# One core, attention plus product-key experts: when weight halves are split and slots are worked off

## The chip, the cores and the metric

The kernel runs on one core of one Trainium2 chip. The metric is the time of one execution on the device in microseconds. Engines are named as in the profile: PE is TensorE (PEld its weight loads), DVE is VectorE, ACT is ScalarE, POOL is GpSimd, SP is SyncE, which here only issues DMAs.

## What is computed

With `xn = layernorm(x)` for x of 2,048 tokens by 512, the output is `x + A(xn) + B(xn)`. A is attention with 32 query heads of 16 and one shared key and value head, and an output projection. B is a product-key mixture of experts:

```
q1, q2 = split(xn @ w_q)                      # 32 heads, 128 + 128
s1, s2 = q1 @ k1.T, q2 @ k2.T                 # 64 scores each
t1, i1 = top 2 of s1;  t2, i2 = top 2 of s2
cand, eidx = t1[a] + t2[b], i1[a]*64 + i2[b]  # 4 candidates
top_s, top_e = top 2 of cand
g = softmax(top_s)
act = gelu(xn . u[top_e])                     # u, v: 4096 x 512
B = sum over heads and k of g * act * v[top_e]
```

Each token uses 64 of the 4,096 experts.

## The kernel before

**Tokens and stages.** Tokens lie in 16 tiles of 128, four tiles to a group. For groups 0 and 1 the experts' rows are gathered; for groups 2 and 3 all experts are computed densely and weighted by gates that are zero where a token does not use an expert. Products run in float16 as a high and a low half; `TERMS` (L208) lists the three products kept: high by high, high by low, low by high.

**The outer loop.** After a start stage, attention runs in 256 steps (loop at L1582, `att_steps` at L1382). A step does four score products with their exponentials on ACT (L448, L455), 16 recorded matmuls of probabilities by values (L465), and around them the work of the other threads. In a step `mid()` comes first (what was put off to ACT and DVE: `ON_ACT`, `LATER`, `LAST`, `BEHIND`, then dots, sums and gathers of slots), then the second pair of scores, then `fill()`, which runs the score thread until a cost planned for this step is used up. `STORES` are run at the head of the next step, so that what is stored inside a store comes two steps later. Every engine works its instructions off in the order in which this loop writes them; nothing reorders them.

**The score thread** (`score_thread`, L1296) goes through the chunks of `SEQ` (L676): a phase (token group) and one of eight chunks of four heads. In phase 0 the folded weights of a chunk (`w_q` times keys) are made first by `wp_make` (L630): transposes into a PSUM tile of `xtile` (tag x, three buffers in all), the high half by ACT (L659), the low half by DVE (L660). Later phases read them back from DRAM a chunk ahead. `item` (L681) does one tile of tokens for one chunk: 12 matmuls (L699) into an `xtile`, then MAX8 and FIND_INDEX8 on DVE (L712, L714). After four items `batch` (L731) turns the two best into gates and expert numbers: sums and the comparison on DVE (L739 to L745), the exponential on ACT one step later, then the gates on DVE (`gates`, L808 to L817 for the dense phases); the expert numbers on POOL, through `G_` (L757). For the dense phases (`ph >= NSP`) this index chain is 15 instructions (L758, L796 to L799 twice, L801 to L806), and its results `df1` and `df2` are transposed on PE by `spread` (L937).

**The dense part** (`dense`, L824) follows the last chunk of phases 2 and 3. It transposes the expert numbers and gates (`spread(0)`, `spread(1)`, then, when the gates have been written, `spread(2)`; L949 to L954). Then 32 groups of 16 token columns (`q`, NQ = 32) form the dense gates: DVE builds one-hot matrices (`onehot`, L969 to L976), PE multiplies them (L1012), ACT and DVE copy out in turn. `dense_on` is 2 in this stage. Then come 32 blocks of 128 experts: 12 matmuls with a block's u half (`activations`, L911), gelu and gate on ACT and DVE (L1107 to L1132), and every four blocks the sums with the v halves (`sums`, L1047; matmuls L1058). Between blocks 2 and 4 up to three output blocks of attention (`block_out`, L559) are put in. `dense_on` is 3 from near the end of the one-hot stage, 1 from block 4 on.

**Splitting.** In phase 2 a block's rows of u and v come by `fetch` (L829; tile `rw`, two buffers) on SP, and are split by `half_split` (L867): a high half on ACT (L874), a low half on DVE (L877), and a store for phase 3, which reads the halves back (L870) instead. `half(b)` puts off the u half of block b to the next `mid()`, `later_split(b)` what is left of it; the latter also queues the rows of block b + 2 two stores later. `SPLITS` (L980) says at which group q which of these is called; later blocks are split from the block loop. A block whose halves are not there makes the score thread stop for the step (L1077). The gates' rows are read back by `first_gates` and `fetch_gates` on SP (L859, L861).

**Slots.** A slot is one gathered pair of u and v rows for a tile of 128 tokens: a gather by POOL (L1180), a dot on DVE (L1192), four small DVE instructions and one tanh for each four slots, and a sum into the tile's accumulator on DVE (L1227). There are 512. How many are due by a step is `pos`, which grows each step by a rate that depends on `dense_on` (L1587 to L1590):

```
if dense_on[0] == 1:
    pos += 2.5 if d < half * 3 // 4 else max(0.0, NSL - pos) / max(half - 3 - d, 1)
else:
    pos += (2.5 if len(IDX) < NC * TPH else 2.3 if 0 <= d - since < 32 else 1.75, 0, 0.5, 1.5, 0.5)[dense_on[0]]
```

`d` is the step, `half` is 256, and `since` is the last step with a dense part. So the rate is 2.5 in phase 0 and in the blocks, 1.75 in scoring, 2.3 in the 32 steps of scoring after a dense part, 0.5 in the one-hot stage; from step 192 on what is left is spread over the steps that are left.

Of the kernel before, what the change touches and what calls it, by code (L numbers as in the profile page):

```python
# [23 lines left out]
P = 128  # L24
# [9 lines left out]
NC = 8  # L34
TPH = GT
NPH = NGRP
NSP = 2
# [23 lines left out]
def tile_kernel(ctx, tc, x, wq, wkv, wo, wqT, kT, uv, ub, vb, out):  # L61
    nc = tc.nc
# [72 lines left out]
    XT, XS, XK, XN, ACC, XP = [], {}, {}, {}, {}, [None]  # L135
# [70 lines left out]
                BULK.append(lambda k=k, xt=xt: nc.sync.dma_start(d_xt[g - 1][k], raw(xt[:])))  # L206

    TERMS = ((0, 0), (0, 1), (1, 0))  # L208

    FIRST = ((0, 0), (1, 0), (0, 1))  # L210
    cols = const.tile([P, 40], F32, name="cols")
# [383 lines left out]
    WC = {}  # L595
# [85 lines left out]
    def item(n_, ti, make=()):  # L681
        ph, c = SEQ[n_]
        nph, nc_ = SEQ[n_ + 1] if n_ + 1 < len(SEQ) else (None, None)
        t = TPH * ph + ti
        g, j = divmod(t, GT)
        b, jb = divmod(ti, BT)
        if jb == 0:
            m8 = small.tile([P, BT, 8, 8], F32, name="m8", bufs=1)
            i8 = small.tile([P, BT, 8, 8], U32, name="i8", bufs=1)
            M8[ph, c, b], I8[ph, c, b] = m8, i8  # L690
        m8, i8 = M8[ph, c, b], I8[ph, c, b]
        p = xtile("psc")

        more = nc_ is not None and not (ph >= NSP and c == NC - 1)
        read = more and n_ + 1 >= NC
        n = 0
        for k in range(KC):
            for a, bb in TERMS:
                nc.tensor.matmul(p, XT[k][:, a, j * P:(j + 1) * P], WC[n_][k][:, bb, :],  # L699
                                 start=n == 0, stop=n == 11)  # L700
# [12 lines left out]
        for s in range(8):  # L713
            nc.vector.max_index(i8[:, jb, s, :], m8[:, jb, s, :], p[:, s * E:(s + 1) * E])  # L714
        if jb == BT - 1:
            batch(ph, c, b)
        yield 3 * UNIT
# [13 lines left out]
    def batch(ph, c, b):  # L731
# [22 lines left out]
            LATER.append(go)  # L754

        fi = T("fi", F32, [P, BT, 8, 2])
        G_ = nc.gpsimd  # L757
# [66 lines left out]
    def dense(DG, after):  # L824
# [144 lines left out]
        def onehot(q):  # L969
            if q < NQ:  # L970
# [9 lines left out]
        SPLITS = {NQ - 18: lambda: later_split(0), NQ - 15: lambda: later_split(1),  # L980
                  NQ - 12: lambda: half(2), NQ - 10: lambda: later_split(2),
                  NQ - 8: lambda: half(3), NQ - 6: lambda: later_split(3),
                  NQ - 4: lambda: half(4), NQ - 2: lambda: later_split(4)}

        def first_gates():

# [87 lines left out]
        for b in range(NB):  # L1074
            wd = []
            if b > 1:
# [6 lines left out]
                for k in activations(b, splits[b][0], p):  # L1083
                    if k == 0:
                        store(lambda b=b: (fetch_gates(b + 1), fetch_gates(b + 2)))
                        if b % 2 == 0 and b > 2:
# [64 lines left out]
            if b % 2 and b > 1:  # L1151
# [423 lines left out]
    with tc.manual_schedule(engines=ENGINES):  # L1575
# [6 lines left out]
        for d in range(half + 24):  # L1582
# [2 lines left out]
            if dense_on[0] != 0:  # L1585
                since = d
            if dense_on[0] == 1:  # L1587
                pos += 2.5 if d < half * 3 // 4 else max(0.0, NSL - pos) / max(half - 3 - d, 1)
            else:
                pos += (2.5 if len(IDX) < NC * TPH else 2.3 if 0 <= d - since < 32 else 1.75, 0, 0.5, 1.5, 0.5)[dense_on[0]]  # L1590

            todo = max(min(int(pos + 0.001), g_next[0]) - d_next[0], 0) if d else 0

# [109 lines left out]
```

## Time and profile before

| what | value |
|---|---|
| three runs | 1809.59, 1810.92, 1815.26 us (median 1810.92) |
| profiled execution | 1814.29 us |
| its span, first to last instruction | 1812.6 us |
| mean granted TensorE clock | 0.985 |
| HBM read, written | 407.36 MB, 56.39 MB |

In time, by the trace: the first attention step's values start at 123 us, the first one-hot stage runs from about 571 to 663, its blocks to about 1025, scoring to about 1345, the second one-hot stage from 1361 to 1445, its blocks to about 1784.

How to read the rows: a row of busy times by stage gives the stretch in us and its length, then for each engine the busy time and the number of instructions in parentheses, the granted clock of TensorE, the busy share of the DMA engines and the GB/s. A row of waits gives the engine and its instruction, what it waited for, the sum of us, how often, and the longest. A row of the timeline gives start, length, engine, line, operation, written and read tiles, and how many instructions were merged; in brackets the idle time before it and what ended it. A row of groups gives a line's instructions with their count, the busy time and mean ns of one, and the idle time ahead of them.

### The profile page before, as it was taken

Reading aid. Unit: us, or ns where it says so; the run is one execution under the profiler, and the core shown is the slowest. Engines: PE = TensorE matmul, PEld = TensorE weight load, DVE = VectorE, ACT = ScalarE, POOL = GpSimd, SP = SyncE. Lnnn points to the kernel's source line nnn. Section 1 sums busy time; section 2 is a strip of 40 time slices with the busy share of each in tenths; the row PEclk is TensorE's granted clock in tenths of the full one; section 3 lists DMA queues with packets and bytes.
Section 4 is the critical chain, followed back from the end, with each engine's and each line's share of the span. In section 5 each row is a group of like instructions: output and inputs, shape, how many; then the busy total and the mean of one; then the engine's idle time right before and its main releaser. Section 6 shows DMA issues by size and latency. Waiting matters only on the chain.

```text
span 1812.6 us, 35046 instructions
## 1 busy us (share of the span) xinstructions
PE 1705.5 (94%) x11070; PEld 601.1 (33%) x11070; DVE 1592.4 (88%) x6337; ACT 1328.8 (73%) x1793; POOL 685.1 (38%) x923
## 2 busy tenths in 40 slices
PE   7989998999998889999999999999998899999998
PEld 3433332333333332333333333332333333333332
DVE  7748898999998976899899899999989868989995
ACT  6467787877767886888888666655667877777774
POOL 1034353445543012344344455445541124544440
PEclk9999999999999999999999999999998999999999
DMA  7378788999764567899999976777443789999893
GB/s 260 125 254 308 264 279 282 316 321 324 270 212 139 169 230 260 284 313 341 302 334 345 330 280 237 237 245 245 149 159 131 224 263 293 324 292 332 290 311 114
DMA packets 257273, 470.98 MB, mean 260 GB/s; under 512 B 107316, under 2 KB 118596, under 8 KB 257084
## 3 DMA queue, kind: packets, MB, share of 16 engines
q0 software_dynamic: 73728, 268.47, 43.2%
q1 hardware_dynamic: 182940, 199.59, 34.4%
q8 instruction: 87, 1.43, 0.3%
q14 instruction: 102, 0.84, 0.1%
q10 hardware_dynamic: 416, 0.66, 0.1%
HBM read 407.36 MB, written 56.39 MB: 256 GB/s over the span
## 4 chain that ended last, share of the span: by engine, by line
PE 58%; DVE 20%; ACT 8%; issue 3%; DMA 3%; POOL 1%; SPq 0%; ACTq 0%; DVEq 0%; another core or an unknown queue 0%; POOLq 0%
PE pv L465 17%; PE sc L448 10%; PE psc L699 10%; PE pout L1058 8%; PE pact L915 7%; ACT pt L455 5%; DVE i L714 4%; DVE xa L1227 3%; DVE m L712 3%; DVE g L1192 3%; PE pwo L565 2%; DVE oh L973 2%; PE pw L644 1%; ACT wk L874 1%; DMA rsb<-dinv 1%
## 5 line engine op out<-in xcount | busy, mean ns | idle before, releaser
L455 ACT ACTIVATE pt<-sc 128x1024 f32<-128x1024 f32 x1024 | 990.1, 1026 | 336.6 <-PE sc L448 299.2
L1180 POOL DMA_INDIRECT g<-in_uv_dram,idx x512 | 544.6, 1064 | 896.7 <-DVE xa L1227 367.8
L465 PE MATMUL pv<-pt,vaug 128*32 128x512 f32 x4096 | 503.6, 610 | 0.0
L1227 DVE SCALAR_TENSOR_TENSOR xa<-g,w,xa 128x512 f32<-128x512 f32 x512 | 372.2, 745 | 0.0
L699 PE MATMUL psc<-wk,xt 128*128 128x512 f16 x1536 | 358.4, 381 | 12.5 <-DVE i L714 7.2
L448 PE MATMUL sc<-qa,kaug 64*128 64x512 f16 x2048 | 325.6, 385 | 40.0 <-ACT pt L455 35.3
L1192 DVE CUSTOM_DVE_ANT_0 g<-g,xa 128x512 f32<-128x512 f32 x512 | 334.3, 682 | 2.6 <-DMA g<-in_uv_dram,idx 2.6
L699 PEld LDWEIGHTS <-xt 128*128 128x128 f16 x1536 | 140.9, 98 | 210.9 <-issue 63.0
L448 PEld LDWEIGHTS <-kaug 64*128 64x128 f16 x2048 | 82.0, 94 | 381.7 <-issue 377.9
L714 DVE FIND_INDEX8 i<-m,psc 128x8 uint32<-128x64 f32 x1024 | 206.4, 222 | 0.0
L465 PEld LDWEIGHTS pv<-pt,vaug 128*32 128x32 f32 x4096 | 108.2, 110 | 259.8 <-issue 259.8
L915 PE MATMUL pact<-xt,wk 128*128 128x512 f16 x768 | 184.3, 385 | 4.2 <-DVE wk L877 3.9
L1058 PE MATMUL pout<-wk,wd 128*128 128x512 f16 x768 | 176.5, 380 | 0.0
L712 DVE MAX8 m<-psc 128x8 f32<-128x64 f32 x1024 | 146.1, 214 | 7.9 <-PE psc L699 7.2
L915 PEld LDWEIGHTS <-wk 128*128 128x128 f16 x768 | 69.6, 99 | 105.3 <-issue 29.3
L1058 PEld LDWEIGHTS <-wd 128*128 128x128 f16 x768 | 73.2, 98 | 93.3 <-issue 9.3
L973 DVE TENSOR_TENSOR oh<-io,tr 128x2048 f16<-128x2048 f16 x64 | 77.9, 1218 | 10.0 <-PE pg L1012 4.7
L714 DVE MATCH_VALUE_LOAD i<-m,psc 128x8 f32 x1024 | 72.1, 70 | 0.0
L1131 DVE SCALAR_TENSOR_TENSOR gy<-gy,pact 128x512 f32<-128x512 f32 x60 | 41.0, 683 | 30.2 <-ACT gy L1130 29.0
L1061 DVE SCALAR_TENSOR_TENSOR da<-pout,cols,da 128x512 f32<-128x512 f32 x72 | 53.3, 746 | 15.3 <-PE pout L1058 14.4
L758 POOL CAST fi<-i 128x64 f32<-128x64 uint32 x32 | 8.2, 257 | 141.7 <-DVE i L714 137.9
L1110 DVE SCALAR_TENSOR_TENSOR gy<-gy,gates 128x512 f32<-128x512 f32 x60 | 41.4, 690 | 22.1 <-ACT gy L1132 17.3
(218 smaller groups left out, 1464.6 us busy)
## 6 DMA issues: line engine op xcount, KB each, us to landing
wk<-dw SPq DMA_DIRECT2D x96, 256.0 KB
wqt<-in_wqT_dram SPq DMA_DIRECT2D x32, 512.0 KB
un<-in_uv_dram SPq DMA_DIRECT2D x16, 1024.0 KB
ds<-wk SPq DMA_DIRECT2D x64, 256.0 KB
gates<-dg SPq DMA_DIRECT2D x64, 256.0 KB
wk<-ds SPq DMA_DIRECT2D x64, 256.0 KB
dg<-gst SPq DMA_DIRECT2D x14, 928.0 KB
dw<-wk SPq DMA_DIRECT2D x32, 256.0 KB
```

The costliest lines, as they stand in the source:

```text
L448: nc.tensor.matmul(p[:, b, :], kaug[o:o + 64, kc * P:(kc + 1) * P], QA[u][o:o + 64, i, :], start=True, stop=True)
L455: nc.scalar.activation(PT[u, kc, i], p, AF.Exp, scale=SCALE)
L465: nc.tensor.matmul(PV[u][32 * j:32 * j + 32, :], vaug[:, kc, :], pt[:, b, :], start=kc == 0, stop=kc == 15)
L699: nc.tensor.matmul(p, XT[k][:, a, j * P:(j + 1) * P], WC[n_][k][:, bb, :], start=n == 0, stop=n == 11)
L712: nc.vector.max(m8[:, jb, s, :], p[:, s * E:(s + 1) * E])
L714: nc.vector.max_index(i8[:, jb, s, :], m8[:, jb, s, :], p[:, s * E:(s + 1) * E])
L915: nc.tensor.matmul(p, us[:, a, k * P:(k + 1) * P], XT[k][:, c, :], start=n == 0, stop=n == 11)
L973: nc.vector.tensor_tensor(out=oa, in0=num(P), in1=bc(0, tb, P), op=OP.is_equal)
L1058: nc.tensor.matmul(p, wd[0][:, a, j * P:(j + 1) * P], vs[:, c, :], start=n == 0, stop=n == last)
L1180: nc.gpsimd.indirect_dma_start(out=gt, out_offset=None, in_=uv, in_offset=bass.IndirectOffsetOnAxis(ap=IDX[ph, c, ti][:, s:s + 1], axis=0))
L1192: nc.vector.tensor_tensor_reduce(u, u, XN[TPH * ph + ti], scale=1.0, scalar=0.0, op0=OP.mult, op1=OP.add, accum_out=a[:, i:i + 1])
L1227: nc.vector.scalar_tensor_tensor(acc, v, w[:, i:i + 1], acc, op0=OP.mult, op1=OP.add)
```

## The change

1. `LOWS_LAST`: the first item of each chunk (`ti == 0`) orders its 12 matmuls anew. A triple is (k, half of x, half of the weights). The high halves of the weights of k = 0, 1, 2 come first, the low halves from the seventh matmul on; the second, third and fourth high half are wanted at the third, fifth and ninth matmul instead of the fourth, seventh and tenth.
2. `G_` is VectorE for the last chunk of the dense phases, so that the index chain of that chunk is written to DVE's queue, behind L745. Twice in the kernel.
3. `SPLITS`: block 0 at group 16 (was 14), block 1 at 20 (17), the u half of 2 at 23 (20), the rest of 2 at 24 (22), the u half of 3 at 26 (24), the rest of 3 at 27 (26). Block 4, at 28 and 30 so far, is split in block 2's activations, block 5 in block 3's instead of at that block's end, behind its output blocks. Rows of block b + 2 are queued behind the split of block b as before.
4. Slot rates: 2.6 instead of 2.5 in the blocks before step 192, 2.3 for 20 steps of scoring instead of 32, 0.25 instead of 0.5 in the one-hot stage.

```
@@ -206,6 +206,8 @@
                 BULK.append(lambda k=k, xt=xt: nc.sync.dma_start(d_xt[g - 1][k], raw(xt[:])))
 
     TERMS = ((0, 0), (0, 1), (1, 0))
+    LOWS_LAST = ((0, 0, 0), (0, 1, 0), (1, 0, 0), (1, 1, 0), (2, 0, 0), (2, 1, 0),
+                 (0, 0, 1), (1, 0, 1), (3, 0, 0), (3, 1, 0), (2, 0, 1), (3, 0, 1))
 
     FIRST = ((0, 0), (1, 0), (0, 1))
     cols = const.tile([P, 40], F32, name="cols")
@@ -695,8 +697,8 @@
         read = more and n_ + 1 >= NC
         n = 0
         for k in range(KC):
-            for a, bb in TERMS:
-                nc.tensor.matmul(p, XT[k][:, a, j * P:(j + 1) * P], WC[n_][k][:, bb, :],
+            for kk, a, bb in LOWS_LAST[n:n + 3] if ti == 0 else [(k, *ab) for ab in TERMS]:
+                nc.tensor.matmul(p, XT[kk][:, a, j * P:(j + 1) * P], WC[n_][kk][:, bb, :],
                                  start=n == 0, stop=n == 11)
                 n += 1
             if read and ti == 0 and k < 2:
@@ -754,7 +756,7 @@
             LATER.append(go)
 
         fi = T("fi", F32, [P, BT, 8, 2])
-        G_ = nc.gpsimd
+        G_ = V if ph >= NSP and c == NC - 1 else nc.gpsimd
         G_.tensor_copy(fi, i8[:, :, :, 0:2])
         fv = fi.rearrange("p t (h s) k -> p t h s k", s=2)
         i1a, i1b, i2a, i2b = fv[:, :, :, 0, 0], fv[:, :, :, 0, 1], fv[:, :, :, 1, 0], fv[:, :, :, 1, 1]
@@ -977,10 +979,9 @@
                 OH[q] = oa, ob
 
         half = lambda b: on_act(lambda: halves.__setitem__(b, half_split(b, 0)))
-        SPLITS = {NQ - 18: lambda: later_split(0), NQ - 15: lambda: later_split(1),
-                  NQ - 12: lambda: half(2), NQ - 10: lambda: later_split(2),
-                  NQ - 8: lambda: half(3), NQ - 6: lambda: later_split(3),
-                  NQ - 4: lambda: half(4), NQ - 2: lambda: later_split(4)}
+        SPLITS = {NQ - 16: lambda: later_split(0), NQ - 12: lambda: later_split(1),
+                  NQ - 9: lambda: half(2), NQ - 8: lambda: later_split(2),
+                  NQ - 6: lambda: half(3), NQ - 5: lambda: later_split(3)}
 
         def first_gates():
 
@@ -1083,7 +1084,7 @@
                 for k in activations(b, splits[b][0], p):
                     if k == 0:
                         store(lambda b=b: (fetch_gates(b + 1), fetch_gates(b + 2)))
-                        if b % 2 == 0 and b > 2:
+                        if b % 2 == 0 or b == 3:
                             later_split(b + 2)
                         if b == 2:
 
@@ -1148,7 +1149,7 @@
                 if out_ready():
                     block_out()
                     yield 3.6
-            if b % 2 and b > 1:
+            if b % 2 and b > 3:
                 later_split(b + 2)
             if b > 4 and b % 4 == 1 or b == NB - 1:
                 n = 4 if b < NB - 1 else 2
@@ -1585,9 +1586,9 @@
             if dense_on[0] != 0:
                 since = d
             if dense_on[0] == 1:
-                pos += 2.5 if d < half * 3 // 4 else max(0.0, NSL - pos) / max(half - 3 - d, 1)
+                pos += 2.6 if d < half * 3 // 4 else max(0.0, NSL - pos) / max(half - 3 - d, 1)
             else:
-                pos += (2.5 if len(IDX) < NC * TPH else 2.3 if 0 <= d - since < 32 else 1.75, 0, 0.5, 1.5, 0.5)[dense_on[0]]
+                pos += (2.5 if len(IDX) < NC * TPH else 2.3 if 0 <= d - since < 20 else 1.75, 0, 0.25, 1.5, 0.5)[dense_on[0]]
 
             todo = max(min(int(pos + 0.001), g_next[0]) - d_next[0], 0) if d else 0
 
```

More of the change, by code (lines that the diff above doesn't have):

```diff
@@ L697, in item @@
         for k in range(KC):
-            for a, bb in TERMS:
-                nc.tensor.matmul(p, XT[k][:, a, j * P:(j + 1) * P], WC[n_][k][:, bb, :],
+            for kk, a, bb in LOWS_LAST[n:n + 3] if ti == 0 else [(k, *ab) for ab in TERMS]:
+                nc.tensor.matmul(p, XT[kk][:, a, j * P:(j + 1) * P], WC[n_][kk][:, bb, :],
                                  start=n == 0, stop=n == 11)
@@ L756, in batch @@
         fi = T("fi", F32, [P, BT, 8, 2])
-        G_ = nc.gpsimd
+        G_ = V if ph >= NSP and c == NC - 1 else nc.gpsimd
         G_.tensor_copy(fi, i8[:, :, :, 0:2])
@@ L979, in dense @@
         half = lambda b: on_act(lambda: halves.__setitem__(b, half_split(b, 0)))
[L980 to L983, printed above, removed]
+        SPLITS = {NQ - 16: lambda: later_split(0), NQ - 12: lambda: later_split(1),
+                  NQ - 9: lambda: half(2), NQ - 8: lambda: later_split(2),
+                  NQ - 6: lambda: half(3), NQ - 5: lambda: later_split(3)}
         def first_gates():
@@ L1085, in dense @@
                         store(lambda b=b: (fetch_gates(b + 1), fetch_gates(b + 2)))
-                        if b % 2 == 0 and b > 2:
+                        if b % 2 == 0 or b == 3:
                             later_split(b + 2)
@@ L1150, in dense @@
                     yield 3.6
-            if b % 2 and b > 1:
+            if b % 2 and b > 3:
                 later_split(b + 2)
@@ L1587, in tile_kernel @@
             if dense_on[0] == 1:
[L1588 removed]
+                pos += 2.6 if d < half * 3 // 4 else max(0.0, NSL - pos) / max(half - 3 - d, 1)
             else:
[L1590 removed]
+                pos += (2.5 if len(IDX) < NC * TPH else 2.3 if 0 <= d - since < 20 else 1.75, 0, 0.25, 1.5, 0.5)[dense_on[0]]
             todo = max(min(int(pos + 0.001), g_next[0]) - d_next[0], 0) if d else 0
```

2 lines of the change are left out of this document (added).

## The prediction

> **What bounds the kernel now.** First the page: TensorE is busy 94% of the span and heads the chain that ended last; VectorE follows.
>
> ```profile
> PE 1705.5 (94%) x11070; PEld 601.1 (33%) x11070; DVE 1592.4 (88%) x6337; ACT 1328.8 (73%) x1793; POOL 685.1 (38%) x923
> PE 58%; DVE 20%; ACT 8%; issue 3%; DMA 3%; POOL 1%; SPq 0%; ACTq 0%; DVEq 0%; another core or an unknown queue 0%; POOLq 0%
> ```
>
> The matmuls stay as many as they were, so an edit can only win TensorE's idle time (1812.6 - 1705.5 = 107 us) and what the clock loses behind it. Second, the waits, TensorE's own:
>
> ```profile
> PE sc L448 <- ACT pt L455: 35.3, 65, 2.0
> PE pg L1012 <- DVE obs L976: 16.0, 16, 1.9
> PE psc L699 <- DVE i L714: 7.2, 6, 2.0
> PE ptd L940 <- POOL da L806: 6.0, 2, 3.4
> PE psc L699 <- DVE wk L660: 4.7, 4, 2.0
> PE pact L915 <- DVE wk L877: 3.9, 1, 3.9
> ```
>
> Third, the busy time by stage, because each of these belongs to one:
>
> ```profile
> core 0: us, PE busy (x) PEld busy (x) DVE busy (x) ACT busy (x) POOL busy (x), PEclk, DMA share, GB/s
> 571.50:663.40 91.90, 74.65 (x906) 30.45 (x904) 88.04 (x157) 78.67 (x99) 7.55 (x6) 0.94 0.50 172
> 663.40:707.00 43.60, 43.60 (x255) 14.57 (x253) 24.05 (x57) 32.98 (x42) 9.96 (x10) 1.00 0.78 260
> 707.00:722.50 15.50, 11.30 (x54) 3.65 (x52) 9.66 (x18) 7.80 (x13) 3.16 (x3) 0.78 0.77 211
> 722.50:1023.00 300.50, 286.86 (x1736) 96.09 (x1734) 272.47 (x637) 247.46 (x339) 119.16 (x109) 0.99 0.96 318
> 1176.80:1254.60 77.80, 71.72 (x438) 23.67 (x438) 76.80 (x490) 45.25 (x57) 42.45 (x79) 0.99 0.69 229
> 1254.60:1345.40 90.80, 90.53 (x557) 30.35 (x555) 89.31 (x592) 57.20 (x70) 44.03 (x88) 0.99 0.59 195
> 1361.50:1444.60 83.10, 70.75 (x866) 29.01 (x864) 78.08 (x140) 69.63 (x85) 10.49 (x8) 0.94 0.58 187
> 1475.50:1784.00 308.50, 306.57 (x1884) 103.19 (x1882) 273.34 (x674) 237.71 (x316) 130.26 (x121) 1.00 0.90 295
> ```
>
> The two one-hot stages (571.5 and 1361.5) leave TensorE idle for 91.9 - 74.65 = 17.3 us and 83.1 - 70.75 = 12.4 us, with VectorE busy 96% and 94%. The scoring from 1176.8 leaves it idle for 6.1 us, with VectorE at 99%. The 15.5 us from 707.0 are one attention step. In the block stages (722.5 and 1475.5) VectorE has 28 and 35 us to spare, and the DMA engines hardly any.
>
> A wait costs more than itself when the clock falls behind it. The worst wait in the one-hot stage lasted 1.91 us; the stretch right after it ran at 0.56:
>
> ```profile
> 649.17 1.01 PE L1012 MATMUL pg<-obs,oh 128*128 128x64 f16 x16 [1.91 <-DVE obs L976]
> ```
> ```profile
> 649.10:655.90 6.80, 6.73 (x57) 2.25 (x58) 6.73 (x12) 3.05 (x5) 1.20 (x1) 0.56 0.89 314
> ```
>
> That loses 6.8 x 0.44 = 3.0 us on top.
>
> **The change, part by part.** The sum is made against the profiled execution, 1814.3 us (its span of 1812.6 and 1.7 around it); the median of the runs, 1810.9, lies 3.4 lower.
>
> **Low parts last: 0.** The 4.7 us of waits on L660 look like its aim. This is the longest of them, ahead of a chunk's first item:
>
> ```profile
> 193.83 2.29 PE L699 MATMUL psc<-wk,xt 128*128 128x512 f16 x6 [1.96 <-DVE wk L660]
> ```
> ```profile
> 193.03 0.75 DVE L660 SCALAR_TENSOR_TENSOR wk<-pwt,cols,wk 128x512 f16<-128x512 f32 x1 [1.15 <-ACT wk L659]
> 197.28 0.75 DVE L660 SCALAR_TENSOR_TENSOR wk<-pwt,cols,wk 128x512 f16<-128x512 f32 x1
> ```
>
> The low part that ended this wait (193.03) is the third of the chunk; the fourth comes at 197.28. The six matmuls that waited read the first two alone. So the wait is not for weights: the item's PSUM tile shares three buffers with the transposes (`xtile`, tag x), and its buffer is free once that third low part has read it. The new order leaves this as it is. The high parts that it wants earlier (the third at the fifth matmul) stand before that low part on ScalarE. Bounds: 0 to 4.7 gained; I take 0.
>
> **Last index chain on VectorE: 0.** The chain of 15 instructions (L758 to L806) leaves GpSimd, and nothing else there is late. On VectorE it is put right behind L745. What is queued behind it: two sums into xa, a block operation, a dot, and then the gates (L809 to L817), for which `spread(2)` waits.
>
> ```profile
> 561.05 0.18 DVE L741 TENSOR_TENSOR c<-m 128x16 f32<-128x16 f32 x1
> 561.33 0.17 DVE L742 TENSOR_TENSOR cond<-c,c 128x16 f32<-128x16 f32 x1
> 561.67 0.18 DVE L745 TENSOR_TENSOR mx<-mx,s 128x16 f32<-128x16 f32 x1
> 565.36 0.25 DVE L817 SCALAR_TENSOR_TENSOR da<-gd,gh 128x32 f32<-128x32 f32 x1
> ```
> ```profile
> 566.75 2.91 PE L940 MATMUL ptd<-ident,da 128*128 128x128 f32 x12 [3.40 <-POOL da L806]
> ```
>
> An instruction that needs the one before it starts 0.28 us after it (561.05 to 561.33). The chain at 15 x 0.1 to 15 x 0.28 takes 1.5 to 4.2 us; about two thirds depend on the one before, so I take 2.8. It ends at about 564.7, where GpSimd released TensorE at 566.75: eight transposes start 2.0 us sooner. The gates move from 565.6 to 568.4, and the last four transposes, done by 569.7 so far, wait for them and end at about 569.2. In the second dense part:
>
> ```profile
> 1349.42 0.18 DVE L817 SCALAR_TENSOR_TENSOR da<-gd,gh 128x32 f32<-128x32 f32 x1
> ```
> ```profile
> 1351.77 1.11 PE L940 MATMUL ptd<-ident,da 128*128 128x128 f32 x4 [0.24 <-ACT tr L941]
> ```
>
> The gates ended at 1349.6 and the last transposes began at 1351.77; 2.8 us later the gates set that start at 1352.4. So 0.5 us won there, 0.6 lost here: one wait is exchanged for the next. I take 0; range from 4 gained (both waits shortened by 2) to 3 lost.
>
> **Splits.** Block 5 is split after the three output blocks of block 3 so far, and its first product waits:
>
> ```profile
> 714.33 4.45 PE L915 MATMUL pact<-xt,wk 128*128 128x512 f16 x10 [3.88 <-DVE wk L877]
> ```
> ```profile
> 735.20:743.40 8.20, 8.20 (x50) 2.97 (x48) 8.19 (x18) 5.14 (x8) 3.70 (x4) 1.00 0.96 296
> ```
>
> The step from 707.0 does one block and one group of sums, as the step from 735.2 does without a wait: 15.5 against 8.2 us, a loss of 7.3 (clock 0.78). Now block 5 is split inside block 3's products, some 25 us earlier (714 less about 689 for its low parts), and block 4 inside block 2's. There (663.4 to 707.0) ScalarE has 10.6 us free and VectorE 19.5, for four castings and four low parts of 0.75 us (below). Their rows must be there:
>
> ```profile
> 661.32 0.33 SPq L832 DMA_DIRECT2D rw<-in_ub_dram  x1
> 670.05 1.28 SPq L859 DMA_DIRECT2D gates<-dg  x3
> ```
>
> SP queued block 5's rows at 661.3, and the first gates 8.7 us later; the split that frees their buffer moves by one group of 16 columns, so they stay ahead of the gates and of their new use at about 683. **-7.3** (3 to 8). What is late next is block 6, split by two instructions on each engine instead of four in that step; I see no wait of more than 1 us. In the second dense part the splits are read back by DMA and no block waits there: 0.
>
> **Slots.** A slot costs VectorE a dot and a sum, 0.65 + 0.73 = 1.38 us; block 4's two low parts leave the first one-hot stage too:
>
> ```profile
> L1227 DVE SCALAR_TENSOR_TENSOR xa<-g,w,xa 128x512 f32<-128x512 f32 x512 | 372.2, 745 | 0.0
> L1192 DVE CUSTOM_DVE_ANT_0 g<-g,xa 128x512 f32<-128x512 f32 x512 | 334.3, 682 | 2.6 <-DMA g<-in_uv_dram,idx 2.6
> L877 DVE SCALAR_TENSOR_TENSOR wk<-rw,cols,wk 128x512 f16<-128x512 f32 x64 | 46.4, 745 | 1.6 <-ACT wk L874 1.6
> ```
>
> The steps are counted by their 16 matmuls on L465:
>
> ```profile
> 571.50:663.40 91.90, 35.62 (x272) 7.45 (x272) 0.94 0.50 172
> 1151.10:1232.60 81.50, 23.08 (x192) 5.00 (x193) 1.00 0.76 244
> ```
>
> *First one-hot stage:* 272/16 = 17 steps at 0.25 instead of 0.5 is 4.25 slots, 5.9 us, and 1.5 for the low parts: VectorE's 88.0 falls to 80.6. ScalarE's 78.7 is then next. If all came through, 7.4 and some clock; TensorE waits for `obs` in bursts and not all along, so I take **-5.5** (0 to 9). *Second:* 16 steps, 4 slots, 5.5 us, no low parts: **-3.5** (0 to 7).
>
> *Scoring after the first dense part:* the rate 2.3 ends 12 steps sooner, in steps 153 to 164 (192/16 = 12), the stretch 1151.1 to 1232.6. That is 12 x 0.55 = 6.6 slots, 9.1 us off a VectorE that is busy 99% from 1176.8 to 1254.6. The 6.1 us of idle time there and 0.8 of clock (77.8 x 0.01) are the most that it can give; the next 90.8 us, at the lower rate, have 0.3 idle. **-5.5** (3 to 7).
>
> *Where they go:* at 81.5/12 = 6.8 us a step, the first block stage has some 45 steps, which take 0.1 more each, 4.5 slots; the other 4.25 + 6.6 + 4 - 4.5 = 10 go to the stage from 1475.5. That is 6 us into 28 free and 14 us into 35 free. I take **+2.5** (0 to 8, for TensorE's waits where a late dot delays a block).
>
> Sum: 0 + 0 - 7.3 - 5.5 - 3.5 - 5.5 + 2.5 = -19.3. From 1814.3 that is 1795.0; 3.4 lower for the median, 1791.6: **1792 us**. For this kernel 0.3% is 5.4 us.
>
> **The rivals.** *A. Only the block wait goes.* ScalarE, or the loop scores, exponential, products, sets the one-hot step, and the waits in scoring come in lumps that move along. Then -7.3 and about +2: 1810.9 - 5.5 = 1805. For it: 35.3 us of TensorE's waits are on L455, and I don't know how many of those would stay. Against: 16.0 are on `obs`, and VectorE's share there is the highest.
>
> *B. The wait is exchanged.* Block 3's first half is now cast about one step after its rows can be queued (two before); if they are late, ScalarE stands with the exponentials behind it. At worst that is as long as the wait it replaces: 1792 + 7 = 1799. Against: the DMA share there is 0.50.
>
> *C. DMA becomes the bound: slower.*
>
> ```profile
> 860.00:1000.00 140.00, 132.96 (x810) 44.16 (x810) 129.03 (x300) 118.41 (x164) 55.57 (x51) 0.99 0.99 326
> ```
> ```profile
> 1261.40:1268.40 7.00, 7.00 (x48) 2.44 (x47) 6.86 (x39) 3.96 (x5) 4.50 (x8) 1.00 1.04 369
> ```
>
> A gather is 128 rows of 1,024 float32, 0.524 MB. The change takes 14.5 of them, 7.6 MB, out of stages with a DMA share of 0.50 to 0.76 into stages at 0.90 to 0.99. If 326 GB/s is the ceiling, 7.6 MB cost 23 us, and two waits for late rows with 3.0 us of clock behind each another 6: 1792 + 29 = 1821. It decides once dots wait for landed rows. Against: these waits sum to 2.6 us (L1192 above), and the stretch from 1261.4 moved 369 GB/s, so 326 is no ceiling.
>
> *D. Short waits don't touch the clock.* The three stages lose 91.9 x 0.06, 83.1 x 0.06 and 0.8 to it, 11.3 us, of which my terms hold about half; without that, 1792 + 5 = 1797. [...] The trace disagrees: 1.91 us of waiting, and 0.56 behind it.
>
> **How the numbers follow.** Forecast 0.58, A 0.20, B 0.08, C 0.10, D 0.04. The forecast's own terms span some 1781 to 1802; A reaches to 1808. So 1781 to 1808 leaves out C and a part of the rest. Faster by over 0.3%: 0.58 + 0.08 + 0.04 and 0.08 of A, 0.78; within: 0.12 of A; slower: 0.10.
>
> **What would show it.** Right: no wait of L915 on L877 and the step of block 5 at about 8 us; `pg` on `obs` below 8 us; `psc` on L714 below 3; `psc` on L660 still near 4.7; `ptd` released by VectorE, at about the same time. Wrong: dots waiting for DMA in the block stages, `gy` or `sc` waits that grow there by over 8 us, a wait on row loads before block 3, or one-hot steps as long as before with VectorE idle.

## The result and the profile after

| | before | after |
|---|---|---|
| median, 6 runs each | 1812.26 us (1809.59 to 1815.46) | 1783.92 us (1783.19 to 1786.19) |
| ratio | | 0.9844, 95% interval 0.983 to 0.9858 |
| profiled execution, its span | 1814.29, 1812.6 us | 1783.53, 1781.7 us |
| mean granted clock | 0.985 | 0.994 |

The change makes the kernel 28 us faster; 19.3 were forecast. The page of the kernel after, its busy times and its chain:

```profile
PE 1690.9 (95%) x11070; PEld 598.6 (34%) x11070; DVE 1592.7 (89%) x6367; ACT 1329.0 (75%) x1793; POOL 680.8 (38%) x893
PE 47%; DVE 31%; ACT 8%; issue 4%; DMA 3%; SPq 1%; POOL 0%; ACTq 0%; DVEq 0%; POOLq 0%
```

The matmuls are as many as before, yet TensorE is busy for 14.6 us less (1705.5 to 1690.9): that is the clock (0.985 to 0.994). It idles for 90.8 us instead of 107.1, which is 16.3 less. Together they are the 30.9 us between the two spans. TensorE's waits in the kernel after (sum of us, times, longest):

```profile
PE sc L450 <- ACT pt L457: 34.4, 62, 2.0
PE pg L1013 <- DVE obs L978: 10.4, 15, 1.6
PE psc L701 <- DVE wk L662: 4.7, 4, 2.0
PE ptd L942 <- DVE da L819: 3.3, 2, 2.1
PE psc L701 <- DVE i L716: 2.8, 3, 1.1
PE ptd L942 <- DVE da L808: 1.2, 1, 1.2
PE ptd L942 <- DVE gy L930: 1.2, 1, 1.2
```

Lines up to the one-hot stage have moved by 2, later ones by 1. The wait of the block products on the low parts (3.9) is gone; `obs` has gone from 16.0 to 10.4, the scores' wait for FIND_INDEX8 (L716) from 7.2 to 2.8; the wait for the low parts (L662) is what it was, to the tenth. The stages, cut at the same steps as in the prediction's table (the scoring row there, 77.8 us, is steps 157 to 167):

```profile
core 0: us, PE busy (x) PEld busy (x) DVE busy (x) ACT busy (x) POOL busy (x), PEclk, DMA share, GB/s
571.40:656.50 85.10, 72.35 (x906) 30.42 (x904) 82.19 (x141) 77.71 (x96) 4.53 (x4) 0.98 0.50 165
701.80:709.40 7.60, 7.60 (x51) 2.73 (x51) 7.25 (x16) 6.29 (x10) 2.77 (x3) 1.00 0.71 170
709.40:1008.00 298.60, 285.24 (x1736) 95.88 (x1734) 278.21 (x655) 247.41 (x341) 124.92 (x114) 0.99 0.99 330
1161.70:1231.30 69.60, 69.60 (x434) 23.41 (x432) 68.53 (x458) 44.81 (x56) 35.28 (x72) 1.00 0.64 213
1336.70:1414.40 77.70, 66.55 (x870) 28.48 (x870) 73.23 (x125) 69.33 (x84) 9.03 (x6) 1.00 0.55 183
```

The step of block 5 has gone from 15.5 to 7.6 us. The first one-hot stage is 6.8 us shorter (91.9 to 85.1), the second 5.4, the scoring 8.2, with no idle time left in it. The whole span, by the steps of attention (worked out from the two traces):

| steps | what | before | after | difference |
|---|---|---|---|---|
| start to 63 | start, weights made, scoring | 571.5 | 571.4 | -0.1 |
| 64 to 81 | first one-hot stage | 96.7 | 90.0 | -6.7 |
| 82 to 88 | first blocks | 54.2 | 48.0 | -6.2 |
| 89 to 133 | other blocks | 306.3 | 304.3 | -2.0 |
| 134 to 183 | scoring, second entry | 332.7 | 323.0 | -9.7 |
| 184 to 200 | second one-hot stage | 88.1 | 82.7 | -5.4 |
| 201 to the end | last blocks, tail | 363.0 | 362.4 | -0.6 |

### The profile page after: what moved, and what is told of

Read it like the earlier page. It is cut to its first block, busy times and chain, and to the rows that moved or that the text cites. A ratio compares the mean times of both kernels' runs of the same rounds, so it can differ in the third digit from the quotient of the medians.

```text
span 1781.7 us, 35035 instructions
## 1 busy us (share of the span) xinstructions
PE 1690.9 (95%) x11070; PEld 598.6 (34%) x11070; DVE 1592.7 (89%) x6367; ACT 1329.0 (75%) x1793; POOL 680.8 (38%) x893
## 3 DMA queue, kind: packets, MB, share of 16 engines
q8 instruction: 87, 1.43, 0.3%
## 4 chain that ended last, share of the span: by engine, by line
PE 47%; DVE 31%; ACT 8%; issue 4%; DMA 3%; SPq 1%; POOL 0%; ACTq 0%; DVEq 0%; POOLq 0%
PE pv L467 14%; PE sc L450 8%; PE pout L1059 8%; DVE i L716 7%; PE pact L917 7%; PE psc L701 5%; ACT pt L457 5%; DVE m L714 5%; DVE xa L1228 5%; DVE g L1193 4%; DVE oh L975 3%; PE pwo L567 2%; PE pw L646 1%; DVE obs L977 1%; DVE obs L978 1%
## 5 line engine op out<-in xcount | busy, mean ns | idle before, releaser
L1181 POOL DMA_INDIRECT g<-in_uv_dram,idx x512 | 550.3, 1075 | 867.2 <-DVE xa L1228 398.0
L467 PE MATMUL pv<-pt,vaug 128*32 128x512 f32 x4096 | 496.2, 602 | 0.0
L1193 DVE CUSTOM_DVE_ANT_0 g<-g,xa 128x512 f32<-128x512 f32 x512 | 335.1, 684 | 12.6 <-DMA g<-in_uv_dram,idx 12.3
L716 DVE FIND_INDEX8 i<-m,psc 128x8 uint32<-128x64 f32 x1024 | 206.9, 226 | 0.0
L714 DVE MAX8 m<-psc 128x8 f32<-128x64 f32 x1024 | 146.3, 217 | 6.5 <-PE psc L701 6.2
L716 DVE MATCH_VALUE_LOAD i<-m,psc 128x8 f32 x1024 | 76.7, 75 | 0.0
L1131 ACT ACTIVATE gy<-pact,cols 128x512 f32<-128x512 f32 x60 | 41.7, 696 | 15.3 <-PE pact L917 14.4
```

The costliest lines, as they stand in the source:

```text
L467: nc.tensor.matmul(PV[u][32 * j:32 * j + 32, :], vaug[:, kc, :], pt[:, b, :], start=kc == 0, stop=kc == 15)
L1181: nc.gpsimd.indirect_dma_start(out=gt, out_offset=None, in_=uv, in_offset=bass.IndirectOffsetOnAxis(ap=IDX[ph, c, ti][:, s:s + 1], axis=0))
L1193: nc.vector.tensor_tensor_reduce(u, u, XN[TPH * ph + ti], scale=1.0, scalar=0.0, op0=OP.mult, op1=OP.add, accum_out=a[:, i:i + 1])
```

## The experiments

Each was compared with runs of the kernel before on the same chip. "Times 1812" is the ratio's difference from 1 as microseconds of this kernel. The run with waits made on purpose, the last one below, was made once (1839.5 us) and has no ratio.

| run | ratio to before (95%) | times 1812 |
|---|---|---|
| low parts last alone | 0.9987 (0.9974 to 1.0001) | -2 (-5 to 0) |
| index chain alone | 1.0007 (0.9991 to 1.0022) | +1 (-2 to 4) |
| splits alone | 0.993 (0.9905 to 0.9955) | -13 (-17 to -8) |
| slots alone | 0.988 (0.9863 to 0.9897) | -22 (-25 to -19) |
| one-hot rate alone | 0.9939 (0.9918 to 0.9959) | -11 (-15 to -7) |
| 20 steps alone | 0.9952 (0.992 to 0.9983) | -9 (-14 to -3) |
| first item in another PSUM tile | 1.009 (1.0058 to 1.0122) | +16 (11 to 22) |
| after, gates behind the chain | 0.9913 (0.9886 to 0.994) | -16 (-21 to -11) |
| after, no sums at the entry | 0.983 (0.9811 to 0.9849) | -31 (-34 to -27) |
| after, still more slots moved | 1.0329 (1.0306 to 1.0352) | +60 (55 to 64) |
| after, 2.5 for 2.6 | 1.0109 (1.0065 to 1.0152) | +20 (12 to 28) |
| *the whole change* | 0.9844 (0.983 to 0.9858) | -28 (-31 to -26) |

The four parts alone add up to -36 against -28 for the whole; the bounds of their intervals add up to -49 and -23, so the two sums agree within the noise.

**Low parts last alone.** The kernel before with the new order of the first item's matmuls:

```
+            for kk, a, bb in LOWS_LAST[n:n + 3] if ti == 0 else [(k, *ab) for ab in TERMS]:
```

> The kernel before with the new matmul order of a chunk's first item alone. Theory (the waits on the low part of wk are for a PSUM buffer that a transpose still holds): time within 2 us of before, and TensorE's waits of psc on that line stay near 4.7 us in 4 places. Rival (they are for the weights): the 4.7 us go, with a clock loss of about 1.7 behind the longest, 6 us in all.

```profile
PE psc L701 <- DVE wk L662: 4.7, 4, 2.0
```

The wait stands as it stood: 4.7 us, four times, 2.0 at most. The theory holds; at most 5 us could hide in the interval.

**First item in another PSUM tile.** If the wait is for a PSUM buffer, another buffer removes it:

```
-        p = xtile("psc")
+        p = stile("psc")[:, 0, :] if ti == 0 and 0 < n_ < NC else xtile("psc")
```

> The kernel before with one edit: the first item of chunks 1 to 7 of the first phase, where weights are being made, puts its scores into a PSUM tile of the tag of the attention scores instead of one that it shares with the transposes. Theory (the 4.7 us of psc on L660 are a wait for the PSUM buffer that the low part still reads, not for weights): the psc wait on L660 falls below 1 us; what is gained is at most 4.7 plus some clock, and the attention scores, which wait for their PSUM tiles themselves (35.3 us on L455), may lose as much in those seven steps: 5 faster to 5 slower. Rival (the wait is for weights): psc on L660 stays near 4.7.

```profile
PE sc L448 <- ACT pt L455: 54.5, 79, 2.1
...
PE psc L699 <- DVE wk L660: 1.7, 2, 0.9
```

The order of the matmuls is that of the kernel before, and the wait falls from 4.7 to 1.7 us: most of it was for the buffer. It did not fall below 1, as was expected. The tile now comes out of the attention scores' buffers, whose wait rises from 35.3 to 54.5, and the run is 16 us slower where 5 was the bound: the buffer was dearer than the wait.

**Index chain alone.**

```
-        G_ = nc.gpsimd
+        G_ = V if ph >= NSP and c == NC - 1 else nc.gpsimd
```

> The kernel before with the last index chain on VectorE alone. Theory (the gates queue behind the chain and take its place): time within 2 us of before; the chain takes 2.7 us, the gates come 2.7 us later, and the transposes ptd wait for the gates. Rival (GpSimd's chain was the bound of both entries): 3.4 and 2.6 us of waits go with a clock loss of 1.7 behind each, 6 to 9 us faster.

```profile
PE ptd L940 <- DVE gy L928: 2.4, 2, 1.2
PE ptd L940 <- DVE da L817: 1.8, 1, 1.8
PE ptd L940 <- DVE da L806: 1.3, 1, 1.3
PE ptd L940 <- ACT tr L941: 1.2, 1, 1.2
```

The 6.0 us of waits for GpSimd have become 6.7 us of waits for four other things: a PSUM buffer that L928 still reads (its tile shares the three buffers of `xtile`), the gates (L817), the chain's last result (L806), the castings (L941). No gain, as forecast. The kernel after shows the same in the first entry, each group of four transposes with a wait of its own:

```profile
563.79 0.63 PE L942 MATMUL ptd<-ident,da 128*128 128x128 f32 x4 [1.24 <-DVE da L808]
565.62 0.66 PE L942 MATMUL ptd<-ident,da 128*128 128x128 f32 x4 [1.20 <-DVE gy L930]
567.43 0.63 PE L942 MATMUL ptd<-ident,da 128*128 128x128 f32 x4 [1.16 <-DVE da L819]
```

**Gates behind the chain.** The kernel after, with the exponential issued at once and the gates right behind the chain:

```
+            if ph >= NSP and c == NC - 1:
+                nc.scalar.activation(ex, mx, AF.Exp, scale=col(I_W + c))
+                gates()
+                return
```

> The kernel after with one edit: for the last chunk of a dense phase the exponential is issued at once and the gates stand right behind the index chain on VectorE, ahead of the two sums, the dot and the casting that stood between. Theory (with the chain on VectorE the start of the dense part is set by the last of chain and gates, with other work of VectorE between them): the two ptd groups behind the gates wait 1 to 2 us less, the sums put off cost nothing: 1 to 3 us faster than the kernel after, that is about 1782 where the kernel before gives 1812. Rival (the exponential's way over ScalarE holds VectorE up with everything behind it): the ptd waits stay at 3 to 6 us in sum and the time is the same or up to 2 us longer.

TensorE and ScalarE in that kernel, at the first entry:

```profile
560.26 0.61 PE L450 MATMUL sc<-qa,kaug 64*128 64x512 f16 x2 [7.38 <-ACT pt L457]
```
```profile
558.99 0.31 ACT L752 ACTIVATE ex<-mx,cols 128x16 f32<-128x16 f32 x1 [9.61 <-DVE mx L747]
559.20 3.75 ACT L457 ACTIVATE pt<-sc 128x1024 f32<-128x1024 f32 x4
```

The rival won, and by more than it said: 12 us slower than the kernel after. A 0.31 us exponential stood at the head of ScalarE's queue for 9.61 us, waiting for VectorE; four attention exponentials stood behind it, and TensorE behind those for 7.38. The `ptd` waits for the gates did go; they cost 3.3 us.

**No sums at the entry.** The kernel after, with the slots' sums left out of the step in which the chunk ends (they come later):

```
+        if ph >= NSP and c == NC - 1:
+            quiet[0] = 2
```

> The kernel after with one edit: in the step in which the last chunk of a dense phase ends, no sums of slots are put out, so that nothing of 1.4 us stands between the index chain and the gates on VectorE; the exponential stays where it is. Theory (in the kernel after the dense part's last transposes start when VectorE has worked off what is queued between the chain and the gates): the second and third group of ptd start 1.2 to 1.5 us earlier in the first dense part, the last group 0.7 to 1.5 in the second; with one half-clock stretch less 2 to 5 us faster than the kernel after, about 1780 where the kernel before gives 1812. Rival (the wait is exchanged once more, for ScalarE's castings or the products that fill the gap): the ptd waits fall, but the step is as long as before, 0 to 1 us.

The kernel after and this one, over the same three steps of the second one-hot stage (184 to 186):

```profile
1336.70:1351.10 14.40, 12.74 (x170) 5.50 (x168) 14.23 (x23) 12.95 (x16) 2.97 (x2) 1.00 0.52 168
```
```profile
1334.50:1352.60 18.10, 14.26 (x170) 5.63 (x168) 16.00 (x26) 13.04 (x16) 4.24 (x4) 0.91 0.59 191
```

The entry steps are shorter, 12.0 to 9.2 us and 9.4 to 8.4. The sums put off then stand in the one-hot steps: three more instructions on VectorE, 3.7 us more. The ratio cannot be told from that of the kernel after, and its interval would also hold a gain of 2 us. By the traces it is one more exchange, of the kind that the rival named, with the lost time further on than it said.

**Splits alone.**

```
+        SPLITS = {NQ - 16: lambda: later_split(0), NQ - 12: lambda: later_split(1),
...
+                        if b % 2 == 0 or b == 3:
...
+            if b % 2 and b > 3:
```

> The kernel before with the new places of the splits alone. Theory: 7 to 9 us faster, 7.3 of it in the one step of block 5 (15.5 to about 8 us), the rest in the first one-hot stage from two low parts that leave it; no change after 750 us. Rival (the wait moves to another block or to the row loads): less than 3 us faster, with a new wait of TensorE or ScalarE between 640 and 720 us.

The step of block 5 falls from 15.5 to 7.6 us (708.7 to 716.2 in its trace); 1.7 come back in step 84, where ScalarE now splits. The median is 10.7 lower and the ratio's figure is 13: more than the wait, with an interval of 9 us.

**Slots, whole and in two parts.** The whole of part 4, then the one-hot rate and the scoring steps by themselves:

```
-                pos += 2.5 if d < half * 3 // 4 else max(0.0, NSL - pos) / max(half - 3 - d, 1)
+                pos += 2.6 if d < half * 3 // 4 else max(0.0, NSL - pos) / max(half - 3 - d, 1)
...
-                pos += (2.5 if len(IDX) < NC * TPH else 2.3 if 0 <= d - since < 32 else 1.75, 0, 0.5, 1.5, 0.5)[dense_on[0]]
+                pos += (2.5 if len(IDX) < NC * TPH else 2.3 if 0 <= d - since < 20 else 1.75, 0, 0.25, 1.5, 0.5)[dense_on[0]]
```

> The kernel before with the three slot rates alone. Theory (VectorE's load bounds the one-hot stages and the scoring after the first dense part): 20 to 23 us faster, about 6 in each one-hot stage, 8 to 9 in the scoring between 1150 and 1260 us; the wait of 3.9 us of pact for block 5 stays. Rival (the parts need each other, the one-hot stage being bound by ScalarE's splits as much): 12 us faster or less.

> The kernel before with one edit: the slot rate in the one-hot stages is 0.25 instead of 0.5. Theory (VectorE sets the pace of the one-hot steps, each slot taken out of them comes through to TensorE nearly whole, and the slots cost nothing in the block stages): first one-hot stage 5 to 7 us shorter, second 3 to 5, the wait of L915 on L877 stays at 3.9, nothing lost in the last stage: 8 to 12 us faster. The prediction's own terms would give 5.5 - 1.5 (low parts) + 3.5 - 1.5 = about 6. Rival (the loop over ScalarE sets the one-hot step): 0 to 3 us faster, and the obs wait stays above 13.

> The kernel before with one edit: the rate 2.3 holds for 20 scoring steps after a dense part instead of 32. Theory (VectorE sets the pace there, and a wait of about 2 us also costs a stretch at half clock, so that more than the idle time is won): scoring of steps 153 to 168 is 7 to 9 us shorter, the psc waits on L714 lose 4 us, and the last stage takes the 6.6 slots more without loss: 7 to 10 us faster. The prediction's own terms would give 5.5 - 1.5 = 4. Rival (the waits there come in lumps that only move to a later step): 0 to 2 us faster, with the sum of the psc waits on L714 above 6.

TensorE's waits in the three, in that order:

```profile
PE pg L1012 <- DVE obs L976: 12.5, 16, 1.8
...
PE psc L699 <- DVE i L714: 1.7, 2, 1.1
```
```profile
PE pg L1012 <- DVE obs L976: 8.0, 13, 1.5
PE psc L699 <- DVE i L714: 7.9, 7, 2.6
```
```profile
PE pg L1012 <- DVE obs L976: 18.7, 22, 1.9
...
PE psc L699 <- DVE i L714: 2.3, 2, 1.2
```

Each rate acts on its own wait: the one-hot rate takes `obs` from 16.0 to 8.0 and leaves L714 at 7.9, the 20 steps take L714 from 7.2 to 2.3 and leave `obs` at 18.7. VectorE sets the pace in both stages, and both rivals are out. Together they give about what part 4 gives. The 20 steps also shorten the second one-hot stage, by 3.3 us (83.1 to 79.8 in steps 184 to 199): its rate was not touched, but the slots that stood in steps 187 and 188 came to others. So some of this is lumps that fall well.

**Still more slots moved, and one part less.** How far is the edge? The kernel after with rates 0 and no step at 2.3; and the kernel after with 2.5 where the change put 2.6:

```
-... 2.3 if 0 <= d - since < 20 else 1.75, 0, 0.25, 1.5, 0.5)[dense_on[0]]
+... 2.3 if 0 <= d - since < 0 else 1.75, 0, 0.0, 1.5, 0.5)[dense_on[0]]
```
```
-                pos += 2.6 if d < half * 3 // 4
+                pos += 2.5 if d < half * 3 // 4
```

> The kernel after with the slots moved further: rate 0 in the one-hot stages (0.25 in the kernel after), and 2.3 for no step of scoring (20). That takes some 4 + 11 + 4 = 19 slots more out of the stages before the last blocks; at 1.38 us each that is 26 us more of VectorE and 10 MB more of gathers in the last stage, where the kernel after has 29 us of VectorE free in 320 us and moves 307 GB/s. Theory (slots are free there only while VectorE has time left): the one-hot stages and the scoring have little left to give, 0 to 4 us; the last stage has VectorE at 98 to 99% and loses 5 to 25 us to TensorE waiting for VectorE's part of the blocks, with the dots' wait for DMA still small: 2 to 22 us slower than the kernel after. Rival 1 (the prediction's C, DMA is the bound): the dots wait for landed rows, over 20 us in sum. Rival 2 (still free): 0 to 4 us faster than the kernel after.

> The kernel after with one part of its slot rates undone: 2.5 instead of 2.6 a step in the first block stage. Some 4.5 slots more are left for the last stage, that is 14.5 more than in the kernel before, where the kernel after has 10 more and the run with rates 0 and no step at 2.3 has 29 more (and lost 95 us). Theory (the price is no rising line but an edge: 12 gather buffers go round from the gather over its landing, dot and sum, and up to some rate of slots their round hides; the dots' wait for landed rows tells how near the edge is: 2.6 us in the kernel before, 12.3 in the kernel after, 80.8 in that run): the dots' wait rises to 15 to 35 us, TensorE's idle time in the last stage by 0 to 6, and the time by 0 to 10 us over the kernel after, that is 1784 to 1794 where the kernel before gives 1812. Rival 1 (the price rises evenly with the slots from the kernel after on, 95 us for 19): 22 us slower. Rival 2 (2.6 cost something in the first block stage): 1 to 3 us faster.

Both were missed by far: 88 and 48 us slower than the kernel after (ratios 1.0329 and 1.0109 against 0.9844) where at most 22 and 10 were expected. In the first, the waits that rival 1 named came (dots waited for rows for 80.8 us, over its 20), but not its cause, a full DMA, and VectorE did not fill up; in the second the edge is there, steeper than either said. VectorE's wait for gathered rows, in the kernel after, with 2.5, and with still more moved (2.6 us in the kernel before):

```profile
DVE g L1193 <- DMA g<-in_uv_dram,idx: 12.3, 17, 1.4
```
```profile
DVE g L1193 <- DMA g<-in_uv_dram,idx: 49.6, 36, 3.7
```
```profile
DVE g L1193 <- DMA g<-in_uv_dram,idx: 80.8, 54, 3.3
```

And steps 209 to 251 of the last stage in the same three:

```profile
1471.40:1748.80 277.40, 275.88 (x1697) 93.11 (x1697) 261.76 (x659) 212.96 (x286) 135.61 (x124) 1.00 0.98 324
```
```profile
1469.60:1780.20 310.60, 287.36 (x1693) 95.05 (x1691) 263.79 (x665) 214.07 (x288) 141.21 (x129) 0.97 0.91 294
```
```profile
1473.90:1838.70 364.80, 302.30 (x1697) 98.08 (x1698) 286.24 (x724) 216.04 (x291) 159.83 (x145) 0.93 0.85 274
```

Neither VectorE (94, 85 and 78% busy) nor the DMA engines (324, 294, 274 GB/s) are fuller in the slower ones. What changes is the distance from a gather to its dot. By the traces, from the start of the k-th gather on GpSimd to the start of the k-th dot, in steps 222 to 234:

| kernel | slots left at step 209 | median | dots in the gather's own step, 1, 2, 3 steps later |
|---|---|---|---|
| before | 120 | 11.2 us | 0, 4, 27, 5 |
| after | 129 | 8.9 us | 0, 24, 15, 0 |
| 2.5 | 134 | 8.0 us | 9, 30, 1, 0 |
| still more | 147 | 8.1 us | 7, 35, 2, 0 |

For dots that waited, this distance is the time to landing: 7.8 to 10.1 us in the kernel after, 4.4 to 10.0 with 2.5. With 12 gather buffers, more slots a step mean that the buffer for a slot comes free later, against the step of its dot. Where the dot comes two steps after its gather, the rows are nearly always there (10 of 176 dots waited, the four kernels together, steps 209 to 251); one step after it 76 of 286 waited, and in the same step 21 of 41, with everything queued behind them on VectorE. 129 slots are on this side of the edge and 134 beyond it, and 5 slots cost 39 us between the profiled spans (1781.7, 1820.9). In all four kernels most gathers of steps 209 to 251 start within 1 us of the end of the sum that frees their buffer, the one 12 slots earlier (90 of 120 before, 99 of 129 after, 95 of 133 with 2.5, 94 of 146 with still more): the buffers do set when a gather starts. But more buffers were not tried, so that their number is the cause of the edge is argued, not shown. One rival is untested: slots come whole. In the kernel after each of these 43 steps holds exactly three dots; with 2.5 eight of them hold four, with still more twenty hold four or five (the kernel before has one step of five). So the edge also lies at three dots a step, and no run separates the two.

**Waits made on purpose.** To test what a wait does to the clock:

```
+        more = 3 + (d_ - 138) // 2 % 3 if 138 <= d_ < 168 and d_ % 2 == 0 and kc % 2 and i else 0
+        for _ in range(1 + more):
```

> The kernel after with ScalarE made late on purpose: in steps 138, 140 up to 166, in which TensorE hardly waits, the last of the four exponentials of a step is done 3, 4 or 5 times more than needed (in turn; the same values written again), 0.97 us each. TensorE's next scores then wait about 1.4, 2.3 or 3.3 us. Theory (the clock is set anew in fixed windows of 3.41 us, whose place differs from one execution to the next: half when TensorE was idle for 1.9 us or more of the window before, full below 1.5): no half-clock window behind the waits of 1.4, behind about half of those of 2.3 and most of those of 3.3, each decided by how the wait lies across the edge of a window; all half-clock stretches start a whole number of 3.41 us apart. [...] Rival 2 (each wait above 1.9 us costs a half-clock stretch, as the prediction took it): behind all of 2.3 and 3.3. Time: 15 waits of 2.3 on average, 35 us, and 1.7 us for each half-clock window.

Two waits of the same length, 2.43 us each, and the windows around them, cut on the grid on which all half-clock stretches of this execution start:

```profile
1061.97 0.39 PE L450 MATMUL sc<-qa,kaug 64*128 64x512 f16 x2 [2.43 <-ACT pt L460]
...
1210.67 0.39 PE L450 MATMUL sc<-qa,kaug 64*128 64x512 f16 x2 [2.43 <-ACT pt L460]
```
```profile
1059.49:1062.90 3.41, 0.98 (x12) 0.38 (x13) 3.18 (x27) 3.35 (x5) 1.24 (x4) 1.00 0.51 154
1062.90:1066.31 3.41, 3.41 (x21) 0.36 (x9) 2.44 (x8) 1.27 (x3) 2.30 (x7) 0.50 0.02 5
1206.26:1209.67 3.41, 1.98 (x10) 0.68 (x9) 3.38 (x29) 3.28 (x5) 1.02 (x1) 1.00 1.03 399
1209.67:1213.08 3.41, 2.41 (x22) 0.62 (x21) 1.37 (x7) 3.06 (x5) 0.00 (x0) 1.00 0.77 294
1213.08:1216.49 3.41, 3.41 (x19) 1.39 (x15) 3.34 (x13) 1.94 (x2) 1.90 (x2) 1.00 0.23 26
```

The first lies whole in one window, 2.43 idle, and the next window has the clock at 0.50. The second lies across an edge, 1.43 and 1.00, and the clock stays at 1.00. Of the 15 waits the five of 1.1 to 1.8 us cost no clock; of the ten from 2.15 to 3.62 nine did. The same length gives both, so the length of the single wait does not decide, and Rival 2 does not hold. These steps grew by 53.6 us: 35.5 of waits and 17 for ten half-clock windows at 1.7 (half of 3.41).

## Why the prediction was right, and where it was off

**The mechanism and the sign were right, and the time lies in the range; it is 8 us below the forecast.** By its own steps:

- *Low parts, 0:* right, -2 with an interval that reaches 0, and the wait is for the PSUM buffer.
- *Index chain, 0:* right, 0.9991 to 1.0022. The working had eight transposes start 2.0 us sooner. Counted from the start of their step (560.1 before, 559.3 after), the first four start 2.2 sooner (at 4.5 us instead of 6.6), the next four 1.4, behind a PSUM buffer that it had not seen, and the last four 0.3, behind the gates. The step is no shorter for it (11.4 us before, 12.0 after): the six products behind the transposes took 2.56 us instead of 1.62, in a window at half clock (568.10 to 571.51).
- *Splits, -7.3:* right, -7.9 in the step itself, -6.2 with what ScalarE gives back in steps 84 and 87. Rival B did not come: no wait for rows. Rival A is out with the slots alone, at -22.
- *One-hot, -5.5 and -3.5:* -6.7 and -5.4. *Scoring, -5.5:* -8.7 in steps 153 to 169, above the 6.9 that the prediction named as the most that it could give.
- *Where the slots go, +2.5:* -2.0 in steps 89 to 133 and -0.3 in steps 201 to 251, no cost at all. Of the 2.0, 1.7 is one half-clock window less: the traces of before and of each part alone have two there, that of after one. The forecast had no such term.

The term that was mis-sized is the clock. The sum kept about half of 11.3 us for it; 14.6 came. The trace of before has 15 windows at half clock between 125 and 1750 us, that of after 5, and ten at 1.7 us are 17, some of it while TensorE waited. Of TensorE's idle time 16.3 us went; the sum without its clock had about 14. Rival D, that short waits leave the clock alone, is refuted by the run with waits made on purpose. The row that the prediction set against it shows less than it says: the half clock began at 648.27, in the middle of the wait of 1.91 that ended at 649.17. In the window before, TensorE was idle for 1.82 us, 0.81 in an earlier wait and 1.01 in this one; what counts is the sum in a window, not the single wait.

**The step that failed, without harm to the number, is the price of more slots in the last stage.** The prediction measured the room there by VectorE's free time ("14 us into 35 free") and gave rival C, DMA, 0.10 with a price by bandwidth. By the runs the price does not come with bandwidth or with VectorE's busy time, which both fall, but with the distance from a gather to its dot, and the edge lies within 5 slots of the kernel after. With 2.5 for 2.6 the change would have been 20 us slower than before. The row that spoke of it was quoted: dots waited for rows for 2.6 us in all, three times; how many steps lay between a gather and its dot was not asked.

Of the marks set for it: no wait of the block products, `psc` on L716 below 3, `psc` on L662 at 4.7, VectorE as the releaser of `ptd`, all as said; `obs` is 10.4 where "below 8" stood. One of its signs of being wrong came too: dots waited for rows in the last block stage for 12.3 us, 2.6 before. It cost nothing there yet (277.4 us for steps 209 to 251, 277.7 before), but it was the sign of the edge.

## What to carry to other kernels

Work moved out of a stage with a full engine pays more than the idle time that it frees, because waits near two microseconds also cost clock (here all 66 windows with 2.0 us or more of idle time had one at half clock behind them, up to 1.7 us lost in each); but measure the room where it goes by the distance between each transfer and its use, since there five slots more cost 39 us while VectorE and the DMA engines were less busy than in the faster kernel. A small instruction that waits for another engine must not be put into an in-order queue ahead of work that many wait for (an exponential of 0.31 us, at two places, cost 12), and a wait that has several causes close behind one another is exchanged, not removed. Try each part by itself before it is called useless or useful: of two that look like side issues here, one gained nothing when added alone (chain), and the other, undone alone, took the whole gain with it (2.6).

## What the runs showed of the hardware

**The granted clock changed in steps of 3.41 us.** In the traces of before and after, each half-clock stretch between 125 and 1750 us has a granted clock of 0.50 and lasts 3.41 us or twice that. In each of the 14 profiled executions all half-clock stretches begin a whole number of 3.41 us apart, and the place of this grid differs between executions: modulo 3.41 it is 3.15 us in that of before, 1.49 in that of after. TensorE's idle time in a window at full clock, and the window that follows it (all 14, 125 to 1750 us):

| idle in the window | windows | half clock in the next |
|---|---|---|
| 0.7 to 1.5 us | 444 | 0 |
| 1.5 to 1.9 | 82 | 33 |
| 1.9 to 2.0 | 27 | 22 |
| 2.0 and more | 66 | 66 |

The counts can shift by a few windows between neighbouring rows with how finely the grid is laid; the first and the last row keep none and all. Several short waits add up within a window (three of 0.4 to 0.6 us, 1.51 in all, ahead of the half clock at 1361.7 in the trace of before), and one wait across an edge may cost nothing (the 2.43 us that ended at 1210.67 in the run with waits made on purpose, 1.43 and 1.00: the clock stayed at 1.00). This also moves the time of one and the same program: up to step 62 the kernel before and the one-hot rate alone run the same instructions, and steps 0 to 61 took 430.9 us in the one trace and 426.9 in the other, with only 0.9 of the difference in TensorE's idle time; the one has two half-clock windows there (194.3 and 293.3), the other none. 2.0 us of idle time in a window were enough for half clock in the next each time (66 of 66).

**Landing is not slower when the last stage is slower.** Rows waited for landed after a median of 8.2 us in the kernel after, 6.9 with 2.5 and 5.9 with still more moved. These are the late rows alone, and a dot that comes sooner also waits for earlier ones. For all gathers of steps 209 to 251 the traces have the DMA packets (144 to a gather, counted off here in order of time, so the times are approximate): from a gather's start to its last packet the median is 5.6 us before, 6.2 after, 5.5 with 2.5, 5.1 with still more. From there to the dot it is 5.4, 3.0, 2.0 and 1.5 us. So the rows do not come later in the slower kernels; the dots come sooner behind them.
